# Mixer layer on one core: x tiles ahead of the head block, a reordered opening, nine of w2's high halves on GpSimd, an early gelu table, first MLP blocks in parts

## The chip, the cores and the metric

One of the eight cores of a Trainium2 chip runs the kernel. The metric is the device time of one execution in microseconds. Before the change it is 425.15 us, the median of three runs (423.82 to 425.76).

## The reference

```python
x = A_x                              # 1 x 2048 x 512, fp32
xn = layernorm(x)
s = attention(xn, wqkv, wo)          # 32 heads of 16, 8 keys at distances 0, 2, ..., 14
g = silu(mlp(xn))                    # mlp: layernorm(xn) @ w1 + b1, gelu, @ w2 + b2; d_ff = 1376
out = x + s * g
```

## The kernel before

Every large product is done in pairs of fp16 halves: an operand is scaled by a power of two taken from its own mean square, the high half is the rounded value and the low half the rest. A product is then three matmuls (high x high, high x low, low x high). So each weight passes through the same steps in the opening: load in fp32, sum of squares (ScalarE Square with an accumulator, L339, L402, L986, or VectorE statistics, L974), a matmul with a matrix of fours that totals over the partitions (`total`, L345), some VectorE instructions of one column that make the scale (`half_exp`, `up`, `down`, L349 to L369), a high half (ScalarE, L376, L413, L1006) and a low half (VectorE, L377, L417, L1009).

The 2048 tokens are cut into 16 tiles of 128, eight of each parity c (a key is an even distance away). For c = 0 `ln0` takes the statistics of a tile (L458, L459), a power on GpSimd (L443), normalises (on VectorE L484 for the groups (2,) and (3,), in `y_act` L462 on ScalarE or again L484 for the groups of two), transposes on TensorE (L491) and splits into halves (L495 ScalarE, L496 VectorE). For c = 1 the transposes are done by DMA.

`qkv(c, hb, u)` makes query, key and value of one parity and one block of eight heads: per tile 12 matmuls of 384 columns (L545) into one of two PSUM buffers `ps`, and one ScalarE eviction (L553) into `U`. There are eight such units u. `attention` works on `U` with VectorE alone, but for three GpSimd sums per unit (L676, L677), an addition of the mask (L607) and an exp on ScalarE. Its output goes through a DMA transpose into `oT` (L641), and is multiplied with wo in `wo_first` and `wo_last` (L723). The MLP runs in 44 steps (four blocks of 512 tokens by eleven f): `mlp1` is 12 matmuls of 512 columns into one of two buffers `mh` (L785), a gelu (L798), the high half (L801) and the low half: for the first eight steps TensorE subtracts the high half in place (L810) and ScalarE reads the rest (L813), after that VectorE does it (L804). `mlp2` (L826) adds four times three matmuls two steps later.

All engines run queues that are fixed when the kernel is built. `Plan` records each operation with an engine, a planned duration and a priority, and `issue` places them one after another by a list schedule; the resulting order per engine is what the hardware executes in order. Loads go through SP in the order in which `Plan` places them; at most eight are under way in its model. The constants PW1, PS2, PW2 and others at the top are priorities of the opening's parts.

The opening before loads the two pieces of wqkv's head block 0 ("q0"), then x tiles 2 and 3, then the pairs (0,1), (4,5), (6,7), then w1, head block 1, w2. GpSimd does 20 memsets first; the last two are L960 and L961.

## Time and profile before

| what | us |
|---|---|
| median of three runs | 425.15 |
| the profiled execution, its own time | 426.52 |
| its span in the trace | 424.7 |
| TensorE busy | 406.7 (96%) |
| VectorE busy | 396.7 (93%) |
| ScalarE busy | 217.6 (51%) |
| GpSimd busy | 97.8 (23%) |

The profiled execution took 1.8 us more than its span (426.52 less 424.7), and 1.4 us more than the median of the timed runs. "Busy" counts instructions from start to end. TensorE and VectorE are both busy nearly all the time, so the page alone doesn't say which of them sets the end; that has to be read in stages. In the trace's rows, PE is TensorE, DVE VectorE, ACT ScalarE, POOL GpSimd, SP the queue that issues the DMAs; "idle before" is how long the engine had nothing to do ahead of the row, with what ended it.

### The profile page before, as it was taken

Reading aid. Unit: us, or ns where it says so; the run is one execution under the profiler, and the core shown is the slowest. Engines: PE = TensorE matmul, PEld = TensorE weight load, DVE = VectorE, ACT = ScalarE, POOL = GpSimd, SP = SyncE. Lnnn points to the kernel's source line nnn. Section 1 sums busy time; section 2 is a strip of 40 time slices with the busy share of each in tenths; the row PEclk is TensorE's granted clock in tenths of the full one; section 3 lists DMA queues with packets and bytes.
Section 4 is the critical chain, followed back from the end, with each engine's and each line's share of the span. In section 5 each row is a group of like instructions: output and inputs, shape, how many; then the busy total and the mean of one; then the engine's idle time right before and its main releaser. Section 6 shows DMA issues by size and latency. Waiting matters only on the chain.

```text
span 424.7 us, 5503 instructions
## 1 busy us (share of the span) xinstructions
PE 406.7 (96%) x2072; PEld 206.6 (49%) x2072; DVE 396.7 (93%) x434; ACT 217.6 (51%) x340; POOL 97.8 (23%) x87
## 2 busy tenths in 40 slices
PE   0999979999999999999999999999999999999995
PEld 0666524445544654445544654455445544444442
DVE  3998999998999979999999999998999999999966
ACT  4799975845376456744466254125312284226400
POOL 5310202002500382002700360046002610250013
PEclk9999969999999999999999999999999999999999
DMA  8964420003241235742162034022423264005325
GB/s 277 412 245 148 146 79 0 2 7 143 85 101 50 100 87 120 129 109 43 54 180 100 0 88 99 2 74 80 155 98 107 69 161 174 0 2 127 122 49 198
DMA packets 43050, 44.83 MB, mean 106 GB/s; under 512 B 27496, under 2 KB 28064, under 8 KB 42768
## 3 DMA queue, kind: packets, MB, share of 16 engines
q1 hardware_dynamic: 43024, 44.49, 34.7%
q8 instruction: 16, 0.26, 0.3%
q14 instruction: 10, 0.08, 0.1%
HBM read 23.53 MB, written 7.34 MB: 73 GB/s over the span
## 4 chain that ended last, share of the span: by engine, by line
PE 84%; ACT 9%; DVE 3%; DMA 2%; issue 1%; SPq 0%; DVEq 0%
PE z L826 27%; PE mh L785 26%; PE ps L545 22%; PE ps L723 6%; ACT w L376 2%; ACT U L553 2%; DMA prod<-in_A_x_dram 2%; ACT w L339 1%; PE z L723 1%; PE mh L723 1%; DVE U L714 1%; DVE U L767 1%; ACT wq L402 1%; ACT yT L495 1%; DVE bn L458 1%
## 5 line engine op out<-in xcount | busy, mean ns | idle before, releaser
L545 PE MATMUL ps<-wq,yT 128*128 128x384 f16 x768 | 129.3, 328 | 0.0
L785 PE MATMUL mh<-yT,w 128*128 128x512 f16 (+1 forms) x528 | 123.5, 385 | 0.9 <-ACT h L813 0.9
L826 PE MATMUL z<-w,h 128*128 128x512 f16 x480 | 112.0, 379 | 0.0
L545 PEld LDWEIGHTS <-yT 128*128 128x128 f16 x768 | 75.5, 99 | 51.1 <-issue 1.5
L785 PEld LDWEIGHTS <-w 128*128 128x128 f16 (+1 forms) x528 | 53.4, 101 | 65.8 <-issue 6.3
L798 ACT ACTIVATE mh<-mh,b1T,hsc 128x512 f32<-128x512 f32 (+1 forms) x44 | 33.0, 749 | 88.0 <-PE mh L785 87.8
L596 DVE TENSOR_TENSOR prod<-U 128x2048 f32<-128x2048 f32 x32 | 74.1, 2317 | 1.0
L826 PEld LDWEIGHTS <-h 128*128 128x128 f16 x480 | 47.1, 98 | 55.3 <-issue 0.3
L599 DVE TENSOR_REDUCE L<-prod 128x128 f32<-128x2048 f32 x32 | 72.9, 2279 | 0.3
L553 ACT ACTIVATE U<-ps,cs 128x384 f32<-128x384 f32 x64 | 37.2, 581 | 67.4 <-PE ps L545 63.4
L653 DVE TENSOR_TENSOR prod<-L,U 128x2048 f32<-128x2048 f32 x28 | 63.4, 2285 | 0.1
L676 POOL COPY gate<-prod 1x1 f32<-1x1 f32 x21 | 4.4, 208 | 210.7 <-DVE prod L596 204.2
L648 DVE TENSOR_TENSOR prod<-prod,prod 128x2048 f32<-128x2048 f32 x16 | 36.5, 2284 | 0.0
L677 POOL TENSOR_TENSOR prod<-prod 128x1024 f32<-128x1024 f32 x14 | 32.9, 2347 | 0.0
L723 PEld LDWEIGHTS <-oT 128*128 128x128 f16 x192 | 18.8, 98 | 22.4
L801 ACT ACTIVATE h<-mh,hsc 128x512 f16<-128x512 f32 x40 | 27.4, 685 | 0.9
L723 PE MATMUL ps<-wo,oT 128*128 128x512 f16 x120 | 26.9, 379 | 0.0
L804 DVE SCALAR_TENSOR_TENSOR h<-mh,hsc,h 128x512 f16<-128x512 f32 x32 | 23.8, 744 | 2.8 <-ACT h L801 2.8
L607 POOL TENSOR_TENSOR L<-L,misc 1x384 f32<-1x384 f32 x8 | 19.4, 2430 | 20.6 <-DVE L L599 20.6
L677 POOL TENSOR_TENSOR prod<-prod,prod 128x1024 f32<-128x1024 f32 x7 | 16.4, 2344 | 0.0
L798 ACT ACT_TABLE_LOAD x12 | 15.4, 1283 | 0.2
L636 ACT ACTIVATE o<-prod,osc 128x1024 f16<-128x1024 f32 (+1 forms) x9 | 9.4, 1050 | 11.5 <-DVE prod L648 6.2
(144 smaller groups left out, 338.1 us busy)
## 6 DMA issues: line engine op xcount, KB each, us to landing
f<-in_A_x_dram SPq DMA_DIRECT2D x31, 256.0 KB, 3.7
U<-U SPq DMA_DIRECT2D x16, 392.0 KB, 3.7
gd<-f SPq DMA_DIRECT2D x12, 256.0 KB, 2.0
oT<-in_B_w_dram SPq DMA_DIRECT2D x2, 1024.0 KB
yT<-in_B_w_dram SPq DMA_DIRECT2D x2, 1024.0 KB
f<-gd SPq DMA_DIRECT2D x8, 256.0 KB, 3.4
out_dram<-f SPq DMA_DIRECT2D x8, 256.0 KB, 2.0
out_dram<-U SPq DMA_DIRECT2D x8, 256.0 KB, 2.3
```

The source lines that it names most:

```text
L545: nc.tensor.matmul(b.t[:, 0:384], y[:, s, k, o:o + P], wq[:, hb, k, t], start=(n == 0), stop=(n == 11))
L553: act(384, lambda i=i, b=b: nc.scalar.activation(U3[:, i:i + 31:15, :], b.t[:, 0:384].rearrange("p (t e) -> p t e", t=3), AF.Identity, sca ...
L596: dve(2048, lambda p2=p2, g=g: nc.vector.tensor_tensor(p2(), q, slots(Ut, KH, 2 * g), op=ALU.mult), qk + [("kh", ub, 0), ("kh", ub, 1), (" ...
L599: dve(2048, lambda pr=pr, g=g: nc.vector.tensor_reduce(L3()[:, 2 * g:2 * g + 2], pr.t.rearrange("p (r f d) -> p r f d", r=2, d=DH), AX.X, ...
L648: dve(n, lambda: nc.vector.tensor_tensor(d(), a(), b(), op=ALU.add), keys, [dkey])
L653: dve(2048, lambda: nc.vector.tensor_tensor(pr.t.rearrange("p (r f d) -> p r f d", r=2, d=DH), L3()[:, 2 * g:2 * g + 2].rearrange("p r (f ...
L677: nc.gpsimd.tensor_tensor(x.t[:, 0:1024], x.t[:, 0:1024], y(), op=ALU.add)
L723: nc.tensor.matmul(b.t, oT[:, hb, i // 4, s, i % 4], wo[:, hb, t], start=(hb == 0 and n == 0), stop=(hb == NHB - 1 and n == 2))
L785: nc.tensor.matmul(b.t[0:M], w1[:, k, s, f * P:f * P + M], yT[ch][:, t, k], start=(n == 0), stop=(n == 11))
L798: act(512, lambda: nc.scalar.activation(b.t[0:M], b.t[0:M], AF.Gelu_apprx_tanh, bias=b1T[0:M, f:f + 1], scale=hsc[0:M, 1:2]), [b, ("b1T",) ...
L801: act(512, lambda: nc.scalar.activation(hi()[0:M], b.t[0:M], AF.Identity, scale=hsc[0:M, 2:3]), [b], [hk])
L826: nc.tensor.matmul(z.t, hl[s][0:K, t * P:(t + 1) * P], w2[0:K, f, w], start=(f == 0 and n == 0), stop=(f == NF - 1 and n == 2))
```

## The change

The text of the change, cut to its core (the planner's own constants and a few renamed keys are left out):

```diff
-LOADS = ["q0", (2, 1), (3, 1), (0, 2), (4, 2), (6, 2)]
+LOADS = [(2, 1), (3, 1), "q0", "q2", (0, 2), (4, 2), (6, 2)]
+BEFORE_W1 = (0, 1, 4, 5)
...
+            self.dma += o.nbytes / (o.rate if self.dma > SLOW else 265e3)
...
-                    if best is None or t < best[0]:
+                    if best is None or (t, o.prio) < (best[0], best[1].prio):
...
+        if n == 2:
+            for k in range(2):
+                pl.add("pe", 0.15, lambda k=k: nc.tensor.matmul(
+                    b.t[:, 0:1], fours, cols()[:, k:k + 1], start=(k == 0), stop=(k == 1)),
+                    [ckeys[k]], [b], prio=min(pl.prio, PTOT))
+            n = 1
...
+    def on_pool(n, hi, src, s, r, w, **k):
+        pool(0.3 + n * POOL1, lambda: nc.gpsimd.tensor_scalar(hi, src(), s, 1.0, op0=ALU.mult, op1=ALU.mult),
+             r, [w], port=False, **k)
...
+        behind = [("yd", i) for i in (2, 3) if n > 1]
         for a in range(n):
-            stats(mv, a, mk[a], xs[a], xkeys[a], **first)
+            stats(mv, a, mk[a], xs[a], [xkeys[a]] + behind, **first)
...
-        for i in IORD:
+        for i in IORD if u else IORD0:
...
+            ends = [1, 2, 3, 4, 8, 12] if u == 0 and i == IORD0[0] else [4, 8, 12] if u < 2 else [12]
+            for n0, n1 in zip([0] + ends, ends):
+                pe(n1 - n0, 384, lambda mm=mm, n0=n0, n1=n1: mm(n0, n1), [("yh" if n1 <= 4 else "y", c, i)] +
+                   [("wq" if n1 == 12 else "wqh", hb, k) for k in range(min(n1, KT))], [b],
...
+        for n0 in range(0, 12, 3) if ch == 0 and f < 3 else (0,):
+            n1 = n0 + 3 if ch == 0 and f < 3 else 12
+            pe(n1 - n0, 512, lambda n0=n0, n1=n1: mm(n0, n1),
...
-        sumsq(lambda k=k: cw1.t[:, k:k + 1], (cw1, k), s1a[:, k], ("s1a", k),
+        sumsq(lambda k=k: cw1.t[:, k:k + 1], (cw1, k), s1a[:, k], [("s1a", k)] + [("y_", i) for i in BEFORE_W1],
...
             split(w2[:, k, 0], w2[:, k, 1], (s2a, s2b)[k // 4][:, k % 4], zsc[:, 0:1],
-                  [("s2", k // 4), ("zsc0",), ("w2j", k // 4), ("yT", 2 + k // 4)], ("w2", k))
+                  [("s2", k // 4), ("zsc0",), ("w2j", k // 4), ("yT", 2 + k // 4)], ("w2", k),
+                  "act" if k < 2 else "pool")
         else:
-            act(512, lambda k=k, K=K, b=b: nc.scalar.activation(
-                w2[0:K, k, 0], b.t[0:K], AF.Identity, scale=zsc[0:K, 0:1]),
-                [b, ("zsc0",), ("w2j", k)], [("w2h", k)])
+            on_pool(512, w2[0:K, k, 0], lambda b=b, K=K: b.t[0:K], zsc[0:K, 0:1],
+                    [b, ("zsc0",), ("w2j", k)], ("w2h", k))
...
+    warm = sb.tile([1, 1], F32, name="warm")
+    act(1, lambda: nc.scalar.activation(warm, ident[0:1, 0:1], AF.Gelu_apprx_tanh),
+        [("y", 0, i) for i in range(NI)] + [("wq", 1, k) for k in range(KT)], [("warm",)], table="gelu")
```

QHI, a switch for high halves of head block 0 on VectorE, is set to 4, so with k below 4 it never applies. The order of tiles in the first unit is now 2, 3, 0, 1, 4, 5, 6, 7 instead of 2, 3, 1, 4, 5, 6, 7, 0.

Since the planner orders every queue, the change moves more than its text says. The queues that result, with the old kernel's line numbers (what is between is unchanged in kind):

```text
SP    x tile 2, x tile 3, q0 (two pieces), x (0,1), (4,5), (6,7), w1, head block 1, w1's rest, w2   (as before from x (0,1) on)
ACT   table, Square q0, copy tile 2, Square q0, copy tile 3, four q0 high halves (L413), normalise 0 and 1, evict (L553),
      ... w1's wide Squares (L339) only behind the fourth eviction (before: ahead of the first) ...
      evictions of unit 1 with: two w2 high halves (L376), GELU TABLE and a 1x1 gelu, w1 high halves 4 x 1024 and 4 x 352,
      two Squares of head block 2 (L402), first gelu (L798), L801, L813
POOL  20 memsets, powers (L443, L452), nine w2 high halves [new], L962, L607, ...
DVE   statistics and normalise of tile 2, then of tile 3, low half of tile 2, total's clamp (L351), low half of tile 3,
      half_exp (L358), statistics of tile 0, up (L364), ...
      first product of attention (L596), w2 low halves 0 to 4, w1 low half 0, w2 low half 5, w1 low halves, first reduce
      (L599), w2 low halves 6 to 10, two products (L596), ...
PE    transposes of tile 2, total, transposes of tile 3, total, unit 0 ...; first MLP block, total of head block 2 (two
      matmuls, with three matmuls of the second block between them), second block, L810, third block, ...
```

Before, all eleven w2 high halves stood on ACT: seven ahead of w1's high halves, one and the three of L1006 behind them and last before the gelu table; the table stood directly ahead of the first gelu, and the Squares of head block 2 behind it. On PE, the third unit of qkv (u = 2) now follows ten MLP blocks instead of nine. At the end of the PE queue, the four groups of three matmuls that need the first half of the last unit's `oT` now stand ahead of the ninth group of nine that doesn't need it, not behind it.

More of the change, by code (lines that the diff above doesn't have):

```diff
@@ L371, in down, with split @@
             [h[1]], [dkey])
[L373 removed]
+    def on_pool(n, hi, src, s, r, w, **k):
+        pool(0.3 + n * POOL1, lambda: nc.gpsimd.tensor_scalar(hi, src(), s, 1.0, op0=ALU.mult, op1=ALU.mult),
+             r, [w], port=False, **k)
+    def split(hi, lo, src, s, r, w, eng="act"):
         get = src if callable(src) else lambda: src
         n = get_n(src)
[L376 removed]
+        if eng == "pool":
+            on_pool(n, hi, get, s, r, (w, "hi"))
+        else:
+            act(n, lambda: nc.scalar.activation(hi, get(), AF.Identity, scale=s), r, [(w, "hi")])
         dve(n, lambda: nc.vector.scalar_tensor_tensor(lo, get(), s, hi, op0=ALU.mult,
@@ L387, in tile_mixer, with k0, load_q @@
     stkey = [[xq0], [("U", 1, 2)], [("yT", 2)], [("yT", 3)]]
-    def load_q(hb):
-        pre = pl.users(stkey[hb])
-        for k in range(0, KT, 2):
+    def k0(hb):
+        return dict(rate=400e3, tail=0.6, issue=0.45) if hb == 0 else {}
+    def load_q(hb, kk=range(0, KT, 2)):
+        pre = pl.users([x for x in stkey[hb] if x is not xq0])
+        for k in kk:
             dma(P * 3072, lambda k=k: nc.sync.dma_start(stq[hb]()[:, k * 384:(k + 2) * 384],
                                                         a_wqkv[hb, :, k * 384:(k + 2) * 384]),
-                [], [("stq", hb, k), ("stq", hb, k + 1)] + stkey[hb], after=pre)
+                [], [("stq", hb, k), ("stq", hb, k + 1)] + stkey[hb], after=pre, **k0(hb))
     def prep_q(hb):
@@ L779, in mlp1, with mm @@
         b = R_mh.new()
-        def mm():
-            n = 0
-            for k in range(KT):
-                for (s, t) in ((0, 0), (0, 1), (1, 0)):
-                    nc.tensor.matmul(b.t[0:M], w1[:, k, s, f * P:f * P + M], yT[ch][:, t, k],
-                                     start=(n == 0), stop=(n == 11))
-                    n += 1
-        pe(12, 512, mm, [("y", c, 4 * j + i) for i in range(4)] +
-           [("w1", k, int(f >= 8)) for k in range(KT)], [b])
+        def mm(n0, n1):
+            for n in range(n0, n1):
+                k, (s, t) = n // 3, ((0, 0), (0, 1), (1, 0))[n % 3]
+                nc.tensor.matmul(b.t[0:M], w1[:, k, s, f * P:f * P + M], yT[ch][:, t, k],
+                                 start=(n == 0), stop=(n == 11))
+        for n0 in range(0, 12, 3) if ch == 0 and f < 3 else (0,):
+            n1 = n0 + 3 if ch == 0 and f < 3 else 12
+            pe(n1 - n0, 512, lambda n0=n0, n1=n1: mm(n0, n1),
+               [("y", c, 4 * j + i) for i in range(4)] +
+               [("w1", k, int(f >= 8)) for k in range(n0 // 3, n1 // 3)], [b],
+               after=pl.users([b]))
         if f < NF - 1:
```

66 lines of the change are left out of this document (37 added, 29 removed).

## The prediction

> **What bounds the kernel now.** I read the busy time by stages first. The columns are the stage, its length, then busy time (and instructions) of TensorE, its weight loads, VectorE, ScalarE and GpSimd, the granted clock, the DMA share and GB/s.
>
> ```profile
> 57.50:62.80 5.30, 5.30 (x14) 2.19 (x14) 5.30 (x3) 2.98 (x8) 0.00 (x0) 0.50 0.00 2
> 62.80:420.30 357.50, 357.49 (x1800) 177.28 (x1800) 341.31 (x290) 165.32 (x237) 84.31 (x56) 1.00 0.30 85
> ```
>
> From 62.8 to 420.3 TensorE never stops, so its amount of work sets the end there; time can be had only in front of 62.8 or behind 420.3 (4.4 us to the span's end, in which the change moves nothing). VectorE has 357.5 - 341.3 = 16.2 us idle in that stretch: it is a close second. TensorE's order of time shows what the first 62.8 us hold:
>
> ```profile
> 11.22 1.94 PE L491 MATMUL z<-ident,f 128*128 128x128 f32 x8 [4.33 <-DVE f L484]
> 12.98 3.39 PE L545 MATMUL ps<-wq,yT 128*128 128x384 f16 x12
> ...
> 24.82 9.91 PE L545 MATMUL ps<-wq,yT 128*128 128x384 f16 x60
> ...
> 48.78 5.34 PE L785 MATMUL mh<-yT,w 128*128 128x512 f16 x24
> 56.23 0.38 PE L810 MATMUL mh<-h,dg 128*128 128x512 f16 x1 [2.10 <-ACT h L801]
> 57.47 5.28 PE L785 MATMUL mh<-yT,w 128*128 128x512 f16 x12 [0.87 <-ACT h L813]
> ...
> 66.24 2.75 PE L785 MATMUL mh<-yT,w 128*128 128x512 f16 x12
> ```
>
> Three losses. It starts at 11.22. It stands still for 2.10 + 0.87 = 2.97 us ahead of the third MLP block. And that block takes 5.28 us; at the granted clock of 0.50 in the stage row it runs at half speed, where the chain of waits gives a later block 2.59 (last row below): 2.69 lost. The chain says who is late:
>
> ```profile
> 2.58 6.67 DMA prod<-in_A_x_dram
> 9.27 1.29 DVE bn L458 x2
> 10.61 0.47 DVE f L484
> ...
> 37.21 0.47 ACT U L553
> 37.68 2.45 ACT w L376 x4
> ...
> 51.95 0.73 ACT w L1006
> 52.70 1.28 ACT L798
> 54.00 0.75 ACT mh L798
> ...
> 66.40 2.59 PE mh L785 x12
> ```
>
> At the start, x pair (0,1) lands at 9.27, and its two statistics stand on VectorE ahead of the first tiles' normalisation. At 52 it is ScalarE: the gelu of a block that was ready at about 48.78 + 2.6 = 51.4 starts at 54.00, behind high halves of w2 and a table load.
>
> **The change, part by part.** *Head.*
>
> ```profile
> 4.43 0.52 POOL L961 MEMSET hlast<- 1x512 f16 x1
> 7.90 1.09 POOL L443 TENSOR_TENSOR lw<-lw,halves 128x1 f32<-128x1 f32 x2 [2.96 <-DVE ssq L351]
> 3.94 0.84 ACT L402 ACTIVATE wq<-prod 128x768 bf16<-128x768 f32 x1 [1.94 <-DMA prod<-in_A_wqkv_dram]
> 8.38 2.13 ACT L413 ACTIVATE wq<-prod,qsc 128x384 f16<-128x384 f32 x4 [2.13 <-DVE qsc L369]
> 6.94 0.69 DVE L458 BATCH_NORM_STATS2 bn<-prod 128x6 f32<-128x512 f32 x1
> ```
>
> The first transfer landed at 3.94; an x tile in its place is smaller, so it lands no later, I take 3.5. Statistics (0.69) end by 4.4, but the power waits for GpSimd's last memset (4.43 + 0.52 = 4.95), takes 0.55, normalising 0.47: tile 2 is transposed from about 6.1, tile 3 from 7.2, in time that was idle. The price is q0: its second piece lands where x tile 3 did, whose statistics began at 6.94, and its Square waits on ScalarE behind the copy of tile 2 until 7.7. Then VectorE's queue has the low half of tile 3 and the statistics of tile 0 (which wait for 9.27) between the steps of the scale, so the scale is ready at about 10.8, not 8.38. Four high halves at 2.13 / 4 = 0.53 let the first matmuls start at about 11.4 and pace them to 13.2. Before, the fourth ended near 12.98 + 4 x 0.28 (3.39 / 12) = 14.1. So 0.9 to 1.9 is won here (the upper end adds the two tiles' transposes that no longer delay anything). Along the evictions some goes back: unit 1's tiles wait for evictions behind w1's Squares, which now come later. I have unit 1 ending at 47.4 to 47.9 instead of 48.78, and take 1.0.
>
> *The gelu.* ScalarE loses nine high halves of 2.45 / 4 = 0.61, 5.5 us, and the table moves to where it waits for w1's scale anyway. But that scale hardly moves:
>
> ```profile
> 40.97 0.15 DVE L364 TENSOR_SCALAR hsc<-s 128x1 int32<-128x1 int32 x1
> L376 ACT ACTIVATE w<-oT,hsc 128x1024 f16<-128x1024 f32 x4 | 4.5, 1153 | 0.0
> 48.69 1.08 ACT L376 ACTIVATE w<-h,hsc 128x352 f16<-128x352 f32 x2
> L402 ACT ACTIVATE wq<-U 128x768 bf16<-128x768 f32 x2 | 1.7, 844 | 0.0
> ```
>
> It still follows the first product of attention and now three low halves on VectorE, so about 41.7. From there: four w1 halves of 1.1 (1.15 less their overlap), four of 0.5, five evictions of 0.47 and two Squares of head block 2 of 0.85, 10.4 in all: gelu near 52, 2 earlier than 54.00, while the block is ready at 50.4. TensorE has the second block to do meanwhile (2.6) and needs gelu and high half (1.25 more) before L810. I get 0.5 us of waiting there and 0.5 at the total of head block 2, which stands in TensorE's queue ahead of the second block and waits for those Squares: 1.0 instead of 2.97. Splitting the first blocks by k only guards against late low halves and moves no work: nothing, as w1's last low half is due near 49, under the first block. With 1.0 of waiting in two pieces I expect the clock to stay at 1.00: 2.69 saved.
>
> The Trainium skill ("TensorE: Matmul & The Clock Gate", "Part 1: The HAM clock gate") halves the clock only after about 3.4 us of idling; here 2.97 in two pieces was enough, so the rule is loose, but by it too a wait of 1.0 costs nothing more.
>
> *GpSimd's nine halves.* No row shows this form. From below, a fill of as many elements; from above, the only other operation with a scalar operand; nearest in bytes, the sum L716:
>
> ```profile
> L960 POOL MEMSET hlast<- 1x512 f16 x1 | 0.5, 520 | 0.0
> L716 POOL TENSOR_TENSOR U<-U,f 128x512 f32<-128x512 f32 x4 | 5.1, 1268 | 32.8 <-DVE U L767 32.7
> 36.07 0.12 DVE L364 TENSOR_SCALAR zsc<-s 128x1 int32<-128x1 int32 x1
> 43.60 2.52 POOL L962 TENSOR_SCALAR hlast<-hlast,hsc 1x512 f16<-1x512 f16 x1 [18.21 <-DVE hsc L369]
> ```
>
> So 0.52 to 2.52; I take 1.27, nine in 11.4 us from the scale (36.07 before, some half a microsecond earlier now) to 47. The fourth (k = 5) is what VectorE's w1 halves wait behind: due at 40.6 (at 2.52 each: 45.6, about a microsecond late), the last at 47 (58, some 2 us late for VectorE, long before the product needs it). L962 behind them is needed by the eleventh step only. Cost: nothing, up to 2.
>
> The Trainium skill ("GPSIMD Engine Reference", "4.1 Engine selection" and 3.1) calls one-input work on GpSimd roughly line rate, 1.03 cycles an element: an estimate of 0.44 us a half, 4 us for nine; the sum would be the same.
>
> *VectorE's share.* TensorE can't be 5.7 ahead if attention doesn't follow.
>
> ```profile
> 37.98 2.28 DVE L596 TENSOR_TENSOR prod<-U 128x2048 f32<-128x2048 f32 x1
> 54.78 2.27 DVE L599 TENSOR_REDUCE L<-prod 128x128 f32<-128x2048 f32 x1
> DVE h L804 <- ACT h L801: 2.8, 3, 2.1
> 411.00:411.50 0.50, 0.50 (x5) 0.20 (x3) 0.00 (x0) 0.00 (x0) 0.00 (x0) 1.00 0.44 86
> 413.65 6.64 PE L723 MATMUL z<-wo,oT 128*128 128x512 f16 x30
> ```
>
> The first product follows unit 0's last eviction, about 0.9 earlier, but one more low half (0.67) comes after it: VectorE is 0.2 to 0.9 ahead. It gets 2.1 more where its longest wait for the MLP vanishes with TensorE ahead. At the end, the last transposed half lands at about 411.2 (the DMA's share in its last half microsecond is 0.44) and is used at 413.65: 2.4 to spare. That is 4.7 to 5.4, against 5.7 needed, with about 10 of the 16.2 idle still to draw on. I count no loss.
>
> **Sum.** 1.0 (start) + 1.97 (wait) + 2.69 (clock) = 5.7. The profiled execution was 426.52 for a span of 424.7; it would be 420.8. It stood 1.4 above the median, so the median goes from 425.15 to 419.4.
>
> **Rivals.** *VectorE sets the end.* The waits inside attention stay: gain 2.4 + 0.2 to 4.7, 420.5 to 422.5. For it: 93% busy and 16.8 dense microseconds from 37.98 on. Against: its idle time.
> *The half clock stays.* If the gelu is a microsecond or two later than I have it, TensorE idles as long as now: 1.0 to 3.0 won, 422.2 to 424.2. For it: the scale of w1 and both Squares stand ahead of the gelu. Against: 5.5 us off ScalarE.
> *The head is worth more.* If the x pair or the total comes earlier than my walk has it, the first matmul starts near 9.9, and the gain is 2.5 instead of 1.0, with half of the 1.0 wait gone: 417.4.
> *Slower: GpSimd and VectorE exclude each other.*
>
> ```profile
> 376.76 1.08 POOL L607 TENSOR_TENSOR L<-L,misc 1x384 f32<-1x384 f32 x1 [0.38 <-DVE L L599]
> 376.79 3.21 DVE L596 TENSOR_TENSOR prod<-U 128x2048 f32<-128x2048 f32 x1
> 44.65 0.65 DVE L952 TENSOR_SCALAR dg<-ident,hsc 128x128 bf16<-128x128 f32 x1
> 45.23 2.47 DVE L377 SCALAR_TENSOR_TENSOR w<-oT,hsc,w 128x1024 f16<-128x1024 f32 x2
> ```
>
> A sum on GpSimd started 0.03 ahead of a product and held it up by its whole 0.93. If each new half does this, VectorE's dense stretch gets 11.4 longer; past the 4.7 it can lose, the end moves: 425.15 + 11.4 - 4.7 = 431.9, and it is slower from a loss of 4.7 on. Against: while L962, an operation of the new kind, ran until 46.12, two low halves took 2.47, 1.24 each, what one takes alone; only the small L952 beside it looks long.
>
> The Trainium skill ("GPSIMD Engine Reference", "8. Key points") speaks for this rival: GpSimd's memory interface is shared, with contention against VectorE operations that read two tensors, which low halves do. The sum above agrees, L962 doesn't.
>
> **How the numbers follow.** Forecast 0.48, VectorE 0.20, half clock 0.12, head 0.12, slower 0.08. The range 416.2 to 423.0 goes from the head case with a microsecond to spare to half of the clock case; left out are the slower case, the rest of the clock case and some 0.04 of tails, 0.18. Half a per cent, about what a measurement here can tell from none, is 423.0 and 427.3. Faster: 0.48 + 0.20 + 0.12 + 0.06 = 0.86; within: 0.07 (the other half of the clock case and a mild slower one); slower 0.07.
>
> **What would show it.** Right: transposes from about 6 and the first L545 matmul near 11.4; the first gelu near 52, under 1.5 us of TensorE idle around the second MLP block and no stretch at clock 0.50; new GpSimd rows near 1.3 with low halves still at 0.74; no TensorE wait from there to the end. Wrong: low halves or products beside GpSimd stretched by a microsecond each, a TensorE wait for `oT` near 405, or the clock row at 0.50 after the first MLP blocks.

## The result and the profile after

The changed kernel takes 426.99 us (median of 20 runs, 425.86 to 428.38), the kernel before 425.39 (20 runs beside them, 423.79 to 427.45): ratio 1.0037, 95% interval 1.0025 to 1.0049. It is 1.6 us slower, where 5.7 us less were forecast. The profiled execution took 427.19 for a span of 425.4.

The profiled execution of the kernel before (426.52) is one of its longer ones, so the two profiles compared below stand only 0.7 apart. Of 94 executions of that kernel timed beside the experiments, 28 have a mean granted clock of 0.992, as the profiled one has, and take 426.5 in the median; 44 have 0.994 to 0.996 and take 425.5; 22 have 0.998 or 0.999 and take 424.0. All 20 of the changed kernel have 0.997 or more. So the half clock of the profile before isn't in every execution, and to be rid of it is worth about 1.4 us in the median (425.4 to 424.0).

TensorE's order of time in the changed kernel comes first (start, length, engine, line, and in brackets the idle time ahead and what ended it), beside three rows of before that the prediction did not need.

```profile
12.67 6.00 PE L583 MATMUL ps<-wq,yT 128*128 128x384 f16 x20 [2.31 <-ACT wq L443]
18.51 1.04 PE L529 MATMUL z<-ident,f 128*128 128x128 f32 x8
19.38 2.11 PE L583 MATMUL ps<-wq,yT 128*128 128x384 f16 x12
...
48.80 2.11 PE L583 MATMUL ps<-wq,yT 128*128 128x384 f16 x12 [0.43 <-ACT U L591]
50.75 2.64 PE L822 MATMUL mh<-yT,w 128*128 128x512 f16 x11
54.12 0.39 PE L822 MATMUL mh<-yT,w 128*128 128x512 f16 x1 [0.73 <-DVE w L404]
...
74.39 2.75 PE L822 MATMUL mh<-yT,w 128*128 128x512 f16 x12
...
82.58 0.38 PE L851 MATMUL mh<-h,dg 128*128 128x512 f16 x1 [0.26 <-ACT h L842]
86.42 0.38 PE L851 MATMUL mh<-h,dg 128*128 128x512 f16 x1 [0.87 <-ACT h L842]
...
108.34 0.38 PE L365 MATMUL ps<-s,fours 128*128 128x4 f32 x2 [0.57 <-ACT wo L352]
...
228.28 0.81 PE L867 MATMUL z<-w,h 128*128 128x512 f16 x3 [0.89 <-ACT f L883]
...
412.35 8.58 PE L761 MATMUL z<-wo,oT 128*128 128x512 f16 x39
```

```profile
17.08 4.06 PE L545 MATMUL ps<-wq,yT 128*128 128x384 f16 x24
...
76.81 2.75 PE L785 MATMUL mh<-yT,w 128*128 128x512 f16 x12
80.05 0.38 PE L810 MATMUL mh<-h,dg 128*128 128x512 f16 x1
```

Three checkpoints tell the story. The first MLP product starts at 50.75 instead of 48.78: 1.97 late. The sixth block of that product starts at 74.39 instead of 76.81: 2.42 ahead, so 4.4 us were won in between. The last product ends at 412.35 + 8.58 = 420.93, before at 413.65 + 6.64 = 420.29: 0.64 late, so 3.1 us were given back behind block six. Of these, the four waits at 82.58, 86.42, 108.34 and 228.28 make 2.59.

The two stretches that the prediction started from, in the view of stretches of the changed kernel (the third number from the end is the granted clock):

```profile
57.50:62.80 5.30, 5.17 (x25) 2.34 (x24) 5.30 (x7) 4.26 (x7) 0.00 (x0) 1.00 0.54 149
62.80:420.30 357.50, 354.91 (x1789) 176.08 (x1787) 346.85 (x290) 164.98 (x238) 81.72 (x56) 1.00 0.31 85
```

The half clock is gone: 1.00 where 0.50 stood. But behind it TensorE has idle time that it did not have before (354.91 busy of 357.50), and VectorE has 5.5 us more to do in the same stretch (346.85 against 341.31 before): work that it no longer finishes in front of 62.8. The groups of VectorE and GpSimd from 36 to 56, and behind them three rows of the order of time (w1's scale, the first gelu, the softmax's exp), show where it fell behind:

```profile
L404 DVE SCALAR_TENSOR_TENSOR w<-yT,zsc,w 128x512 f16<-128x512 f32 x6 | 6.0, 1003 | 0.0
L404 DVE SCALAR_TENSOR_TENSOR w<-oT,hsc,w 128x1024 f16<-128x1024 f32 x4 | 5.7, 1453 | 0.0
L985 DVE SCALAR_TENSOR_TENSOR s<-s,s 128x1 f32<-128x1 f32 x1 | 0.5, 518 | 0.0
...
L394 POOL TENSOR_SCALAR w<-yT,zsc 128x512 f16<-128x512 f32 x6 | 7.9, 1342 | 11.6 <-DMA U<-U 11.6
```

```profile
44.41 0.14 DVE L384 TENSOR_SCALAR hsc<-s 128x1 int32<-128x1 int32 x1
54.55 0.75 ACT L839 ACTIVATE mh<-mh,b1T,hsc 128x512 f32<-128x512 f32 x1 [0.25 <-PE mh L822]
78.54 0.63 ACT L661 ACTIVATE L<-L 128x512 f32<-128x512 f32 x1
```

GpSimd's halves take 1.34 in the mean, close to the 1.27 taken. VectorE's low halves beside them take 1.00 instead of 0.74, the wide ones 1.45 instead of 1.27. The mean of GpSimd hides what happens; one by one, from 38 to 43, the rows are these:

```profile
38.29 0.70 POOL L394 TENSOR_SCALAR w<-yT,zsc 128x512 f16<-128x512 f32 x1 [11.56 <-DMA U<-U]
38.96 2.80 POOL L394 TENSOR_SCALAR w<-yT,zsc 128x512 f16<-128x512 f32 x1
38.96 2.32 DVE L634 TENSOR_TENSOR prod<-U 128x2048 f32<-128x2048 f32 x1 [0.71 <-DMA U<-U]
41.28 1.02 DVE L404 SCALAR_TENSOR_TENSOR w<-yT,zsc,w 128x512 f16<-128x512 f32 x1
41.74 1.12 POOL L394 TENSOR_SCALAR w<-yT,zsc 128x512 f16<-128x512 f32 x1
```

The first half, with VectorE idle beside it, takes 0.70. The second starts together with a product of VectorE (L634) and ends 0.48 behind it. From the third on, the halves and VectorE's low halves take turns, at 1.0 to 1.1 each. So the two engines wait for each other: GpSimd for nearly the whole of a VectorE operation, VectorE for some 0.3 us of each half.

### The profile page after: what moved, and what is told of

It is laid out like the page before. It is cut to its first block, busy times and chain, and to the rows that moved or that the text cites. A ratio compares the mean times of both kernels' runs of the same rounds, so it can differ in the third digit from the quotient of the medians.

```text
span 425.4 us, 5512 instructions
## 1 busy us (share of the span) xinstructions
PE 407.4 (96%) x2080; PEld 206.5 (49%) x2080; DVE 401.0 (94%) x427; ACT 213.5 (50%) x332; POOL 108.3 (25%) x96
## 4 chain that ended last, share of the span: by engine, by line
PE 72%; DVE 11%; DMA 7%; ACT 6%; issue 2%; SPq 1%; DVEq 0%; ACTq 0%
PE z L867 22%; PE ps L583 20%; PE mh L822 20%; PE ps L761 6%; DVE prod L634 3%; PE z L761 2%; DVE L L637 2%; DMA prod<-in_A_x_dram 2%; DMA h<-in_B_w_dram 2%; DVE prod L691 2%; DVE w L404 2%; DMA yT<-in_A_wo_dram 1%; ACT U L591 1%; ACT w L403 1%; PE mh L761 1%
## 5 line engine op out<-in xcount | busy, mean ns | idle before, releaser
L822 PE MATMUL mh<-yT,w 128*128 128x512 f16 (+1 forms) x528 | 121.8, 379 | 0.9 <-DVE w L404 0.7
L634 DVE TENSOR_TENSOR prod<-U 128x2048 f32<-128x2048 f32 x32 | 74.0, 2315 | 1.7 <-DMA U<-U 0.7
L478 POOL TENSOR_TENSOR lw<-lw,halves 128x2 f32<-128x2 f32 (+2 forms) x6 | 5.1, 854 | 35.4 <-DVE lw L480 28.0
```

Source lines behind the costliest of these rows:

```text
L634: dve(2048, lambda p2=p2, g=g: nc.vector.tensor_tensor(p2(), q, slots(Ut, KH, 2 * g), op=ALU.mult), qk + [("kh", ub, 0), ("kh", ub, 1), (" ...
L822: nc.tensor.matmul(b.t[0:M], w1[:, k, s, f * P:f * P + M], yT[ch][:, t, k], start=(n == 0), stop=(n == 11))
```

## The experiments

The checkpoints of every run, in us of the profiled execution: start of the first MLP product's first and sixth block, end of the last product, all from TensorE's order of time. Median and ratio are of the timed runs.

```
kernel                                   first   sixth  last end   median   ratio [95%]
before                                   48.78   76.81   420.29    425.39
changed                                  50.75   74.39   420.93    426.99   1.0037 [1.0025, 1.0049]
1  changed, q0 issued first              52.91   76.55   422.54    428.48   1.0066 [1.0041, 1.0092]
2  changed, halves replaced by fills     53.61   76.25   421.63    427.22   1.0045 [1.0027, 1.0063]
3  before, halves on GpSimd              48.68   72.61   423.25    428.75   1.0076 [1.0051, 1.0100]
4  before, gelu table first              48.90   72.61   417.96    424.33   0.9967 [0.9951, 0.9983]
5  changed, no GpSimd halves             50.08   72.72   417.53    423.92   0.9963 [0.9947, 0.9979]
6  4 + three low halves later            48.80   72.91   417.99    424.00   0.9965 [0.9949, 0.9981]
7  6 + three high halves later           49.33   72.58   418.10    423.86   0.9955 [0.9940, 0.9970]
8  changed, w2's tail later              51.10   74.07   421.43    427.53   1.0047 [1.0026, 1.0067]
9  before, head alone                    50.82   80.33   424.70    429.94   1.0096 [1.0073, 1.0118]
10 before, all but the head              49.91   72.77   420.68    427.00   1.0038 [1.0022, 1.0055]
11 7 + wo's sum earlier                  49.38   73.55   417.58    423.69   0.9953 [0.9936, 0.9971]
12 changed, TensorE kept busy            49.58   73.22   419.30    425.55   1.0005 [0.9988, 1.0022]
13 11, TensorE kept busy                 48.28   72.33   416.37    422.34   0.9925 [0.9909, 0.9941]
14 before, VectorE held up               48.60   76.59   422.18    430.16   1.0114 [1.0089, 1.0139]
```

### 1: only the order of the first transfers undone

```diff
 (in the changed kernel, as the order is written out)
+        at = [n for n, (t, o) in enumerate(order) if o.eng == "sp" and o.nbytes][:4]
+        for n, x in zip(at, [order[at[m]] for m in (2, 3, 0, 1)]):
+            order[n] = x
```

> The changed kernel with one thing undone: the four first transfers are issued in the old order (both pieces of q0, then x tiles 2 and 3); every other instruction stands where the change puts it. Theory H (the head costs time: q0 behind the x tiles lands at 7.3 instead of 3.9, and the matmuls then start thin and cold): scale of q0 ready near 9 instead of 11.8, four first matmuls of unit 0 by 13.5 instead of 14.8, unit 1 ends at or before 49.8 instead of 50.75, and the time is 0.8 to 1.5 us below the changed kernel, 1.000 to 1.002 of the kernel before. Theory G (the loss is VectorE's lateness from GpSimd's halves): unit 1 may end earlier, but the waits near 82, 85 and 107 stay at 0.3 to 1 us each and the time stays within 0.5 us of the changed kernel, 1.003 to 1.005.

Both missed: it got 1.5 us slower. ScalarE's order of time says why:

```profile
3.91 0.84 ACT L435 ACTIVATE wq<-prod 128x768 bf16<-128x768 f32 x1 [1.91 <-DMA prod<-in_A_wqkv_dram]
...
10.04 0.59 ACT L536 CAST yT<-z 128x512 f16<-128x512 f32 x1 [5.20 <-PE z L532]
10.53 0.85 ACT L435 ACTIVATE wq<-prod 128x768 bf16<-128x768 f32 x1
```

q0 is there at 3.91 again, but its second Square stands behind the copy of the first tile, which now comes at 10.04. The queues are written for tiles first; the transfers alone can't be undone.

### 2 and 5: the changed kernel without GpSimd's halves

In 2 the places of the nine halves were zeroed by GpSimd itself, in 5 ScalarE filled six of them while it waited for q0. In both the second MLP product is so without these high halves.

```diff
-        pool(0.3 + n * POOL1, lambda: nc.gpsimd.tensor_scalar(hi, src(), s, 1.0, op0=ALU.mult, op1=ALU.mult),
+        pool(0.3 + n * POOL1, lambda: None,
...
 (2, at 27 us)
+    pl.fill = lambda: [nc.gpsimd.memset(w2[:, k, 0], 0.0) for k in range(2, NF)]
 (5, ahead of everything on ScalarE)
+    for k in range(2, 8):
+        nc.scalar.activation(w2[:, k, 0].rearrange("p (a b) -> p a b", a=4),
+                             fours.unsqueeze(1).broadcast_to([P, 4, P]), AF.Copy)
```

> The changed kernel without GpSimd's nine high halves of w2: their places are set to zero by GpSimd between 27 and 36 us (so the second MLP product lacks the high halves of w2 from k = 2 on, and the low halves hold the whole value); all else, VectorE's low halves among it, stands where the change puts it. Theory G (GpSimd's halves slow VectorE's two-input work beside them): the low halves of 512 go back from about 1.05 to 0.745 us, the wide ones from 1.43 to 1.27, w1's scale comes by 42.5 instead of 44.41, the second product of attention at 58.5 to 59.5 instead of 61.48, the waits of TensorE at 82, 85 and 107 fall from 2.2 us in all to under 1, and the time is 1.5 to 3 us below the changed kernel: 0.997 to 1.000 of the kernel before. Rival Q (it is the new order of the queues, whatever GpSimd does): low halves may shrink, but the late waits stay and so does the time, 1.003 to 1.005. Rival X (no shared port at all): low halves stay at 1.05 without GpSimd.

> The changed kernel again without GpSimd's nine high halves, now with their places filled by ScalarE while it waits for q0 at 2 to 7 us (constants instead of the high halves of w2 for k = 2 to 7, what the Squares leave for k = 8 to 10; the second MLP product is so not the reference's). Nothing runs on GpSimd from 27 to 46 us, and every other instruction stands where the change puts it. Theory G: low halves of 512 at 0.745 and wide ones at 1.27; w1's scale at 41.5 to 42.5 instead of 44.41; second product of attention at 58 to 59 instead of 61.48; TensorE's waits at 48.05, 53.0, 81.9 and 85.2 (2.9 us in the changed kernel) fall under 1.0; time 2 to 3 us under the changed kernel, 0.9965 to 0.999 of the kernel before. Rival Q (order of the queues alone): low halves short, but the waits at 82 and 85 and the time stay, 1.003 to 1.005.

Run 2 was spoiled by its own fills. This is VectorE's order of time in it, while nine fills ran on GpSimd from 27.04 for 4.27 us:

```profile
27.20 4.13 DVE L573 TENSOR_SCALAR cs<-cT,qsc 128x2 f32<-128x2 f32 x1
```

An operation of two columns stood still until the last fill was done, and TensorE was 3.7 us behind the changed kernel at 43.6, 0.4 at 27. So its 1.0045, which lies in Q's range, says nothing for Q. Run 5 has no such stretch. Its groups of VectorE from 36 to 56, then the moments that answer to those of the changed kernel:

```profile
L403 DVE SCALAR_TENSOR_TENSOR w<-yT,zsc,w 128x512 f16<-128x512 f32 x7 | 5.2, 745 | 0.0
L403 DVE SCALAR_TENSOR_TENSOR w<-oT,hsc,w 128x1024 f16<-128x1024 f32 x4 | 4.9, 1274 | 0.0
...
L984 DVE SCALAR_TENSOR_TENSOR s<-s,s 128x1 f32<-128x1 f32 x1 | 0.2, 154 | 0.0
```

```profile
43.36 0.15 DVE L384 TENSOR_SCALAR hsc<-s 128x1 int32<-128x1 int32 x1
75.77 0.63 ACT L660 ACTIVATE L<-L 128x512 f32<-128x512 f32 x1
83.66 0.38 PE L850 MATMUL mh<-h,dg 128*128 128x512 f16 x1 [0.20 <-ACT h L841]
```

Every low half takes its old time, exp starts 2.8 us earlier (75.77 against 78.54), the waits at 54, 82 and 228 are gone, that at 86 shrinks from 0.87 to 0.20 (the one behind 105 stays, at 0.72), and the kernel takes 423.92: 3.1 us less than the changed one, though VectorE's and TensorE's queues are the same. So G holds, and Q falls. w1's scale stays above the 41.5 to 42.5 of the expectation: 43.36 is what the reordering alone makes of it.

### 3: GpSimd's halves alone

```diff
 (in the kernel before, ScalarE's places kept, k = 2 to 10)
+            nc.gpsimd.tensor_scalar(hi, src, s, 1.0, op0=ALU.mult, op1=ALU.mult)
...
+                  "pool" if k >= 2 else "act")
```

> The kernel before with one part of the change alone: the same nine high halves of w2 (k = 2 to 10) are issued on GpSimd instead of ScalarE, at the places at which they stood; nothing else moves. Theory G: VectorE's low halves beside them take about 1.05, its attention falls 2.5 to 3 us behind (the reduce of 54.78 comes after 57), w1's last wide low half ends near 51.5 instead of 48.9 and TensorE waits some 2 us for it in the first MLP block, while the gelu comes near 52 and no stretch runs at clock 0.50; the sum of both: 0.993 to 0.999. Rival X (GpSimd costs VectorE nothing): low halves 0.745, first MLP block without a wait, gelu at 51.4 when its block is ready, 5 us won: 0.986 to 0.990. Rival E (they exclude each other): VectorE 9 us or more late, 1.005 or more.

VectorE fell as far behind as G says: the reduce due at 54.78 came at 57.41. The gelu came at 52.01, and TensorE was 4.2 us ahead at the sixth block. Then, in TensorE's, ScalarE's and the stages' view:

```profile
80.24 0.59 PE L816 MATMUL mh<-h,dg 128*128 128x512 f16 x1 [4.23 <-ACT h L807]
```

```profile
76.20 0.63 ACT L629 ACTIVATE L<-L 128x512 f32<-128x512 f32 x1
```

```profile
80.40:85.70 5.30, 5.30 (x13) 1.82 (x12) 5.30 (x5) 3.27 (x6) 0.00 (x0) 0.50 0.00 0
```

All of it went back in one wait of 4.23, and the half clock came with it. 1.0076 is outside G's range: G had the stretch and not the tie behind it. It lies in the range of E, but VectorE was 2.6 us late, not the 9 that E needs.

### 4, 6, 7 and 11: the gain without GpSimd, and who takes it back

```diff
 (4: as ScalarE's first instruction)
+    nc.scalar.activation(warm0, fours[0:1, 0:1], AF.Gelu_apprx_tanh)
 (6: low halves of w2 for k = 8 to 10 emitted behind 96 us; 7: their high halves at 67; 11: wo's sum ahead of the reduction)
+MOVED = {"hi8": 67.5, "lo8": 94.2, "wo": 101.9}
+            late = [x for x in order if x[1].tag == tag]
+            order = [x for x in order if x[1].tag != tag]
+            n = next(i for i, x in enumerate(order) if x[0] > at)
+            order[n:n] = late
```

> The kernel before with one added instruction: a gelu of one element as ScalarE's first, while it waits for the first transfer, so that the gelu table is the one that is loaded first; nothing else moves. ScalarE's other functions of the first 50 us use no other table in the trace, so no second load is due until exp. The first gelu should come 1.28 earlier, near 52.7. Theory C (the half clock follows from the length of the idle time, 2.97 before, about 1.7 now): no stretch at 0.50, 3.2 to 4 us won, 0.991 to 0.9925. Rival: the clock still halves, 1.3 won, 0.996 to 0.998. Rival B (what is won at the gelu is paid back by waits later, as in the changed kernel): 0.999 to 1.001, with new TensorE waits behind 80.

> The kernel before with the gelu table first, and VectorE's three low halves of w2 for k = 8 to 10 (2.06 us, at 52.8) moved behind its last low half of head blocks 2 and 3 at about 96; they are needed behind 120. Theory V (what TensorE gains in front of 60 is given back where ScalarE's queue waits for VectorE's scale and softmax at 71 to 76: with the table first 3.9 us were won by 62 and 1.88 lost at 75.6): exp starts about 2 us earlier than 73.9, the TensorE wait at 75 falls under 0.4, and the time is 1.4 to 2.2 us below the run with the table alone, 0.992 to 0.9935. Rival W (the wait at 75 is ScalarE's own: two table loads and its halves in a row): VectorE is 2 us earlier there but the wait stays over 1.2 and the time at 0.996 to 0.9975.

> The kernel before with the gelu table first and both halves of w2 for k = 8 to 10 moved back: ScalarE's three high halves (1.96 us, straight ahead of the first gelu) to where it waits for VectorE at 67 to 71, VectorE's low halves to 96. The first gelu should then start when its block is ready, near 51.4 instead of 52.7, and the waits of TensorE at 53.9 and 54.9 (1.85 with the table alone) fall under 0.7. Theory V: TensorE is 5 us ahead at 62 and VectorE 2 us, so some 1 us of wait comes back at 75, as the old slack there was 2 us: 0.990 to 0.9925. Rival W: wait of 2.5 to 3 us at 75, 0.994 to 0.9965.

> The kernel before with the gelu table first, both halves of w2 for k = 8 to 10 moved back as in the run before it, and one small instruction of VectorE (the sum over the four columns of wo's Squares, 0.15 us, for which TensorE waited 1.5 us near 105 there) moved ahead of the reduction in front of it. Theory V (VectorE's line is the limit wherever TensorE waits on it; each wait is a place in its queue): the wait near 105 falls under 0.2, and if no other one takes its place the time is 1.2 to 1.7 us below the run without this move, 0.9915 to 0.993. Rival N (the next place in VectorE's line takes over): the same time as without it, 0.995 to 0.9965, with a new TensorE wait between 107 and 140.

In 4 the clock stays at 1.00 and 4.2 us are won by the sixth block (72.61 against 76.81), as C says; 1.9 of them are lost again, and the time, 0.9967, misses C's range. The two rows that matter, of ScalarE and of TensorE:

```profile
73.68 0.63 ACT L625 ACTIVATE L<-L 128x512 f32<-128x512 f32 x1
```

```profile
77.72 0.38 PE L812 MATMUL mh<-h,dg 128*128 128x512 f16 x1 [1.72 <-ACT h L803]
```

77.72 - 73.68 = 4.04. That is ScalarE's queue behind exp: a table load, a gelu, a high half of wq, the high half of h. The same 4.04 stands between exp and the waiting product in run 3 (80.24 - 76.20) and in the changed kernel (82.58 - 78.54). So at this place TensorE is tied to VectorE's softmax, and in the kernel before its product came at 80.05 where 73.88 + 4.04 = 77.92 would have done: a slack of 2.1.

Run 6 takes 2.06 us off VectorE ahead of that place, and the wait is gone, as V says and W does not. But VectorE now does them at 96, and its waits row, the only new one, is

```profile
PE ps L554 <- DVE s L358: 1.4, 1, 1.4
```

a small sum that stands behind a reduction in VectorE's queue near 105. The time is that of run 4: V's place was right, its 1.4 to 2.2 us were not. Run 7 is caught at the same place (1.5), and misses V's range too. In run 11 that sum stands earlier and the wait is gone, but a new one of 0.4 comes at 121.84 for a low half on VectorE, as N says; the last product ends 0.5 us earlier than in run 7 (417.58, 418.10), of which the timed runs show nothing clear (0.9953 and 0.9955). TensorE's gain of 3.3 to 4.2 us by the sixth block is worth 2.2 to 2.7 at the end in all four. These are gains on the profiled execution before, with its half clock. The medians of the four, 423.7 to 424.3, are within 0.4 us of the 424.0 that the kernel before takes where its granted clock stays at 0.998 or more: what an earlier gelu leaves at the end is about what the half clock cost.

### 8: the changed kernel, relieved in the same way

```diff
 (and hi8 on ScalarE instead of GpSimd)
+MOVED = {"hi8": 70.0, "lo8": 95.21}
```

> The changed kernel with both halves of w2 for k = 8 to 10 moved: the high halves from GpSimd at 46 to 50 to ScalarE where it waits at 69 to 72, VectorE's low halves from 59.5 to behind 95. GpSimd keeps six. Theory G with V: w1's wide low halves lose their stretch (0.5 to 0.9 us), VectorE is 2.6 to 3 us earlier at the softmax of 78.5, the TensorE waits at 81.9 and 85.2 (1.45 in all) fall under 0.4, that at 53.0 shrinks by half; w1's scale stays near 44.4, since the six halves in front of it stay; time 1.3 to 2.3 us under the changed kernel, 0.998 to 1.0005. Rival Q: the waits stay within 0.3 of what they were, 1.003 to 1.005.

A miss. VectorE was 2.7 us earlier at the softmax (qsc at 73.59, before the move 76.25), but ScalarE's order of time shows who stands in front of exp now:

```profile
74.20 1.93 ACT L1056 ACTIVATE w<-f,zsc 128x512 f16<-128x512 f32 x3
...
78.15 0.63 ACT L668 ACTIVATE L<-L 128x512 f32<-128x512 f32 x1
```

The three halves went to a place where ScalarE had less idle time than I took. exp starts at 78.15, 0.4 earlier than without the move, and the product behind it at 82.19: 4.04 again, and the wait with it. A new wait of 1.1 for a low half on VectorE comes at 181.93. Q's numbers came true here (the same waits, 1.0047), but for this other reason, so the run decides nothing between G and Q; it shows the tie once more.

### 9 and 10: the head alone, and all but the head

```diff
 (9: every part of the change but on_pool, the early table and the MLP blocks in parts; 10: these three alone; both planned anew)
```

> The kernel before with the head part of the change alone (order of the first transfers, split total, high halves of q0 on VectorE where the change has them, tile order of unit 0, Squares of w1 behind the tiles), planned anew; w2's high halves stay on ScalarE, the gelu table is loaded at the gelu, the MLP blocks are whole. Theory H (the change's head loses instead of winning 1.0): first matmuls from 12.5 thin and at the cold clock until 17, TensorE some 0.9 us behind the kernel before at 20 us, and VectorE about 1 us behind at the first product of attention (39 instead of 37.98); the wait at the gelu and the half clock stay as they were, so 1.002 to 1.005. Rival P (the prediction's: the head wins 1.0 and the loss is elsewhere): 0.997 to 0.998.

> The kernel before with the other parts of the change alone (nine high halves of w2 on GpSimd, early gelu table, first MLP blocks in parts), planned anew; the head as before. Theory G with H: the contention is there as in the changed kernel (low halves near 1.05 beside GpSimd, VectorE 3 to 4 us late at the second product of attention: near 60.5), the waits of the changed kernel at 80 to 110 come back in some form (1.5 to 3 us), but it starts 0.9 us better: 0.999 to 1.002, some 1 us below the changed kernel. Rival P: without the head's win it is 1.0 us slower than the changed kernel, 1.006.

The head alone is worse than H says. The first MLP product starts 2.0 us late, ScalarE's gelu 3.3 late, and TensorE waits longer for it than before:

```profile
59.40 0.42 PE L841 MATMUL mh<-h,dg 128*128 128x512 f16 x1 [3.24 <-ACT h L832]
```

The kernel is 4.4 us behind at the end. Without the head the other parts gain 4.0 by the sixth block and lose all of it behind: TensorE's waits in run 10 are

```profile
PE ps L352 <- ACT wo L346: 1.3, 1, 1.3
PE ps L559 <- DMA yT<-f: 1.0, 1, 1.0
PE ps L559 <- ACT U L567: 1.0, 2, 0.7
PE mh L827 <- ACT h L818: 0.6, 2, 0.4
```

So it is not 1 us better than the changed kernel, as expected, but the same: what arrives earlier waits longer. Both were planned anew, so their queues are not parts of the changed kernel's, and their losses don't add up to its.

### 12 and 13: TensorE kept busy ahead of its first products

```diff
+    pl.keep_busy = lambda: [nc.tensor.transpose(R_mh.tiles[0][:, 0:P], ident, ident) for k in range(18)]
 (13: in run 11's kernel, behind q0's total; 12: range(10), in the changed kernel, at the same place)
```

> The changed kernel with ten added transpositions of the identity (128x128, into a PSUM buffer that nobody reads) on TensorE, behind the total of q0 and ahead of the first product, where TensorE waits from 10.36 to 12.67; nothing else moves. Theory K (after an idle stretch TensorE's first 4.3 to 4.7 us of work run at half pace, 0.32 us a matmul of 384 columns instead of 0.16, though the granted clock reads 1.00; the change took the cheap transpositions out of that time, so ten matmuls pay for it): matmuls at 0.16 from 15 on instead of from 17.34, the transpositions of the third and fourth tile at 17 to 17.5 instead of 18.51, unit 1 ends 0.7 to 1.4 earlier than 50.75, and the time is 0.3 to 1.4 us under the changed kernel, 1.0005 to 1.003, as some of it is given back behind 78. Rival M (the pace is set by something else at that time, the DMA traffic or the weight loads): still 0.32 until 17, time unchanged, 1.003 to 1.005.

> The fastest order so far (the kernel before with the gelu table first, w2's last three pieces later and the sum of wo's Squares earlier) with eighteen added transpositions of the identity on TensorE between 6.9 and 10.7, where it waits. Theory K: the first transpositions and twelve matmuls run at full pace (0.11 and 0.16), but the transpositions of the next two tiles wait for ScalarE's normalised tiles of 15.4 and 16.1, so only 0.4 to 0.7 us remain at 17; 0.9935 to 0.995. Rival M: unchanged pace, 0.995 to 0.9965.

TensorE's first microseconds of work run at half pace. These are two stretches of a microsecond of the kernel before (the third number from the end is the granted clock, the next the DMA share; x counts what lies in the stretch, in part too), then the starts of runs 11 and 13:

```profile
13.00:14.00 1.00, 1.00 (x5) 0.49 (x5) 0.84 (x2) 0.59 (x1) 0.41 (x1) 1.00 1.02 410
19.00:20.00 1.00, 1.00 (x8) 0.59 (x6) 1.00 (x6) 1.00 (x4) 0.12 (x1) 1.00 1.07 429
```

```profile
12.85 4.02 PE L555 MATMUL ps<-wq,yT 128*128 128x384 f16 x12
```

```profile
6.43 4.08 PE L1081 MATMUL mh<-ident 128*128 128x128 f32 x18
...
12.74 2.20 PE L559 MATMUL ps<-wq,yT 128*128 128x384 f16 x12
```

In the kernel before the products start 0.32 us apart until 15.5 and 0.16 apart from 15.7 on. The column says 1.00 in both stretches, in the first only because the trace has nothing there: its record of the granted clock begins at 15.59, with 1.00, and the column counts what has no entry as full speed. The record begins at 17.39 in the changed kernel, 16.94 in run 11 and 12.14 in run 13, and the pace doubles at that moment in each. So K holds; the DMA share is about the same in both stretches, so DMA traffic, which M names, is not what sets the pace. With the eighteen dead transpositions the first twelve products take 2.20 instead of 4.02; the first MLP product starts 1.1 us earlier than in run 11, and the kernel takes 422.34. That is more than was expected (0.9925 against 0.9935 at best), and the fastest here, with nothing of the computation left out. In run 12 the twenty products take 5.61 instead of 6.00, so 0.4 comes from the pace; q0 also landed 1.0 earlier in its profiled execution (6.31 against 7.31), and how much of the 1.4 us of its median is which I can't tell.

### 14: how late VectorE may be

```diff
 (in the kernel before, behind the second product of attention)
+    pl.extra = lambda: [nc.vector.tensor_reduce(spare, w1[:, 0:2, 0, 0:1024], AX.X, ALU.add) for k in range(2)]
```

> The kernel before with two added reductions on VectorE (128x2048 of the finished w1 into a spare of two columns, some 2.2 us each) at about 59, behind the second product of attention; nothing else moves, and TensorE keeps its order. Theory V (VectorE has only about 2.0 us to spare where ScalarE's queue waits for its softmax at 72 to 76, and 2.3 us near 105): of 4.4 us of lateness 2.0 to 2.5 reach the end, as TensorE waits near 78 and 105: 1.0045 to 1.0065. The prediction's count (VectorE can lose 4.7 before the end moves): 0.999 to 1.001, without a new TensorE wait.

VectorE's added work, then TensorE:

```profile
58.99 4.59 DVE L1071 TENSOR_REDUCE spare<-w 128x2 f32<-128x2048 f16 x2
```

```profile
81.94 0.38 PE L813 MATMUL mh<-h,dg 128*128 128x512 f16 x1 [1.95 <-ACT h L804]
```

exp started at 77.90, and 77.90 + 4.04 is 81.94. It was 4.02 late (before 73.88) and TensorE waited 1.95 for it: a slack of 2.1, as by the tie, and not the 4.7 of the prediction. At the end 1.9 us remain (420.29 to 422.18). The median, 1.0114, lies above what either theory expected: the profiled execution is the shortest of six (428.41, the longest 432.06), none of the others has a profile, and why they are longer is open.

## Why the prediction was wrong

The forecast was 419.4 and the result 426.99, 7.6 more. By the terms of the sum, 3.0 of it lie at the start, 0.2 at the gelu and the clock, 3.1 in what was given back behind block six, for which the sum had nothing, and 1.2 in its last step: it took the 1.4 between the profiled execution and the median off the changed kernel too, where they are 0.2 (427.19 and 426.99). That difference belongs to the clock term, as above, and was counted twice.

- **The start (1.0 won): wrong, 1.97 lost.** Tile 2 was right: landed by 3.55 (3.5 forecast), transposed at 6.23 (6.1). q0 was not. Its first piece landed at 7.31, after both tiles, so the second tile's transpositions came at 8.75 (7.2 forecast) and the scale at 11.77 (10.8). The first product started at 12.67 (11.4). Then the walk took 0.28 us a product from a row of before; the four first ones now start at the pace of ScalarE's halves, and all pay the slow pace: 20 products and the eight transpositions among them were done at 19.38, before at 17.08 + 8 x 4.06 / 24 = 18.43. The slow pace lasted to 17.39, before to 15.59; how long it lasts differs between executions too (14.20 to 17.24 in the eight profiles with the old head, 17.20 to 18.65 in five with the new one and no added transpositions). The rest of the 1.97 came in small pieces, the wait of 0.43 at 48.80 among them. Experiment 9 shows that the head alone loses 2.0 here and 4.4 in the end.
- **Gelu and clock (1.97 + 2.69 = 4.66 won): right, in size and for the most part in cause.** 1.97 + 2.42 = 4.4 were won between the two checkpoints, and the clock stayed at 1.00. But in the median the clock is worth less than 2.69, as the result shows. The gelu itself came at 54.55, not near 52. ScalarE was idle for 0.25 ahead of it: it waited for its block, and the block's last product for VectorE's low half of w1 (0.73 at 54.12), which hangs on a scale of 44.41 instead of 41.7. Of the two waits of 0.5 that were forecast neither came; this one of 0.73 stood in their place, so the 1.0 taken for waiting was near by luck.
- **GpSimd's halves (nothing, up to 2): wrong, 3.1.** Their time came out right by luck (1.27 taken, 1.34 measured for the six full ones from 36 to 56, 11.8 in all for nine): one alone takes 0.70, the rest is waiting for VectorE. The mistake was the choice between L607 and L962: I took L962, with one partition, as the row for the new kind. Run 5 shows what nine halves of 128 partitions cost: 0.26 on each low half, 0.18 on a wide one, 2.6 us of VectorE in all (6 x 0.26 + 4 x 0.18 + 0.36), and 3.1 us of the kernel. The rule of the Trainium skill ("GPSIMD Engine Reference", "8. Key points") that the prediction weighed, that GpSimd shares its memory interface with VectorE operations that read two tensors, agrees with the runs in kind. The rival built on it had the mechanism and not the price: a half holds VectorE up for some 0.3 us, not for its whole 1.27, so its 11.4 us were four times too large.
- **VectorE (no loss): wrong, and with it the sum.** I added slacks of different places: 0.2 to 0.9 at attention's first product, 2.1 at a wait for the MLP, 2.4 at the end. A lead is spent at the first place where TensorE takes something that hangs on VectorE. That is exp, at 73.88, with 2.1 to spare. With VectorE where it was, the forecast lead of 5.7 there would have met a wait of 5.7 - 2.1 = 3.6, or 2.7 to 3.4 with the 0.2 to 0.9 that the prediction gave VectorE. Experiments 4, 6, 7 and 11 have no halves on GpSimd and still keep only 2.2 to 2.7 of 3.3 to 4.2.
- **The rivals.** "VectorE sets the end" named the mechanism and put it 20 in 100 with a gain of 2.6 to 4.7; with the contention taken out (run 5) it is what happens, at 1.6 gained, the head's loss included. The slower case was the right engine pair with the wrong price, and it did not need 4.7 us of loss to be slower, as 4.7 was never there. The half clock did not stay, and the head was worth less and not more.

## What to carry to other kernels

Before counting a gain of the bounding engine, find the next place where it takes something from a nearly full engine, through a third engine's queue too, and read how long that thing had lain ready: that number is the cap, and the slacks of later places do not add to it. Work moved to an idle engine can have a price on another one that works beside it; read single rows and not means to find it, and measure it once with the moved work taken out, all queues kept. Idle time at TensorE's start is worth filling, and work that seems free there may be what takes it through its slow stretch. And when a profile and a median differ, look at what the profiled execution has that the others lack, before a term of the sum is read from it.

## What the runs showed of the hardware

- GpSimd's scaling of 128x512 float32 to float16 takes 0.70 us with VectorE idle and 2.80 beside a VectorE product of 2.32 (the changed kernel at 38.96). Beside it VectorE's two-input form of the same size takes a third longer (0.745 to 1.003), and a product of 128x2048 in run 3 took 2.71 instead of 2.28. The Trainium skill ("SBUF — State Buffer", "SBUF: two separate sides") has an exclusive lock here, between a VectorE operation with two inputs and a GpSimd operation that reads: the instruction that starts second waits for the whole of the first. The halves agree on GpSimd's side; VectorE lost 2.6 us to nine of them, some 0.3 each and not 0.70.
- GpSimd's fills stop a VectorE operation with a single tensor altogether (4.13 us until the ninth fill was done, where the changed kernel has 0.22). It did not get its turn between two fills, as the low halves do between two halves; why is open.
- TensorE's start: products of 384 columns start 0.32 us apart until the trace's record of the granted clock begins (15.59 in the kernel before), 0.16 apart after that. The Trainium skill ("TensorE: Matmul & The Clock Gate", "Part 1: The HAM clock gate") says that the first 3.4 us or so of work after idling run at half the clock, whatever the work is. The traces agree on the half; in the kernel before it lasts 4.4 us from the first transposition at 11.22. Run 13's transpositions from 6.43 to 10.51 paid that time instead of the products, and its record begins at 12.14. The clock column of the profile does not show this stretch.
- A wait of 4.23 us halved the granted clock in run 3 and one of 3.24 in run 9, one of 1.95 did not (run 14); before, 2.97 in two pieces did. In the four profiles that have it (before, 3, 9, 14) the half clock lasts 6.83 us each time, before from 56.55 to 63.37. In these four records full clock lasts 40.96, 64.85, 341.33 or 361.81 us until the next switch: all multiples of 3.413, as 6.83 is. So the clock seems to switch on a grid of 3.41 us. Where the grid lies against the kernel would then decide whether 2.97 us in two pieces halve it, which would fit the three kinds of executions of the kernel before; no run shows that.
